# Retention, then a gated MLP, on one core: the fifth chunk of batch 0 loaded with the other four, and the first weight load issued one step sooner

## The chip, the core and the metric

The kernel runs on one core of one Trainium2 chip. The metric is the device time of one execution, in microseconds (us). The kernel before takes 321.57 us (median of three runs, 321.35 to 321.59). The profiled execution that all views below come from took 321.33 us.

## What is computed

Inputs are `q`, `k`, `v` (8 batches, 8 heads, 576 positions, 64 wide, all f32) and the weights `w_in` (512 x 2048) and `w_out` (2048 x 512). Cut to what matters:

```python
scores = scale * np.matmul(q, k.transpose(0, 1, 3, 2))
Dmat = np.where(rel >= 0, gamma[:, None, None] ** rel[None, :, :], 0.0)
ret = np.matmul(scores * Dmat[None, :, :, :], v)          # per batch and head
x = ret.transpose(0, 2, 1, 3).reshape(B * S, H * D)       # 4608 x 512
h = x @ w_in
out = (h * np.cos(h)) @ w_out                             # 4608 x 512, f32
```

## The kernel before

**Retention in chunks.** The 576 positions of a batch are cut into five chunks `r` = 0 to 4: four of 128 positions and a last one of 64. For each chunk, k and v are loaded from HBM in f32 to staging tiles (`load`; dst tiles `kn`, `vn`), k is cast to bf16 into `kqb` (`cast`, the instruction at L339) and v is multiplied by the decay into `vb` (`vmul`, L328). `turn_k` transposes a chunk of k on TensorE (PE) into a PSUM bank, and ACT or DVE copies it into `kqt` (L387). `turn_q` does the same for q. `scores` multiplies k by q into two PSUM banks, which DVE masks into `rt` (`mask`, L451). `rest` adds the output of the chunk in one PSUM bank from the running state `sb` and from `rt` and `vb`, updates the state in the bank `st` (copied by ACT to `sb`, L494), and copies the output to `xt` (L501). The outputs of all chunks stand one after another in `xt`, the input of the MLP.

**The MLP in blocks.** The 4608 tokens are cut into nine blocks `j` of 512. `mlp1(j, dt)` makes one of 16 slices of 128 hidden features: four matmuls, a sine on ACT (L526, the cosine), a product on DVE (L529). `mlp2` makes the output of 128 tokens in four parts of four matmuls each; part `p` reads the slices 4p to 4p+3 and the p-th quarter of `w_out`. `w_in` comes in four loads too, each for four values of `dt` (`WI`).

**Who loads what.** SP issues the k, v and q loads (`load`, L278; `load_q0`, L287) on one hardware queue (q1 in the profile). The weights and the q of batch 1 need a cast on the way, and POOL (GpSimd) issues them on its own queue (q0): `w_in_load` (L307), `w_out_load` (L314), `load_qx` (L301). Both queues feed the same 16 DMA engines. Each engine executes its instructions in program order, so a wait in POOL's or SP's list holds back all that stands behind it there.

**The order at the start** is written out by hand in `emit`. Block 0 of the MLP needs the tokens 0 to 511, the chunks 0 to 3 of batch 0. The fifth chunk of batch 0 is needed only by block 1 and is worked in between slices of `mlp1(0, dt)`: `turn_k(0, 4)` after dt 6, `scores(0, 4)` after dt 8, `rest(0, 4)` after dt 10. Before that, PE bridges waits with dummy matmuls (`spin`). SP's loads of chunk 4 wait for the first `w_in` load to have landed (`after=w[:1]`), and SP's loads of batch 1, which come next in SP's list, for the fourth (`after=w[3:]`). In POOL's list the two operations of chunk 4 (`casts(0, 4)`) stand between the four `w_in` issues and the four `w_out` issues; the casts of batch 1 follow the latter.

**PSUM banks.** There are eight: two for scores (`SC`), one for outputs (`PO`), one for the state (`ST`) and four (`MM`) which `bank()` hands out in turn. A group of matmuls that gets a bank waits until the last reader of the bank is done. PE has one instruction list, and a group waits at its first matmul for all that it reads and for its bank.

During block 0's `mlp2`, q, k of batch 1 are turned and its first chunks are worked (`turn_q(1, c)` after n = 7, `turn_k(1, 0)` after n = 9, and so on). From batch 2 on the transposes are DMA transposes (L350), and the loads run ahead of the compute.

Of the kernel before, what the change touches and what calls it, by code (L numbers as in the profile page):

```python
# [123 lines left out]
class _Kernel:  # L124
# [468 lines left out]
    def emit(self):  # L593
        s = self.s
        self.load("k", 0, 0)
        self.load_q0()
        for x, r in (("k", 1), ("v", 0), ("k", 2), ("v", 1), ("k", 3), ("v", 2), ("v", 3)):
            self.load(x, 0, r)
        self.consts_a()
        for c in range(NP):  # L600
            self.consts_b(c)
        self.consts_n()
        self.cast("pool", 0, 0)
        for c in range(NP):
            self.cast_q0(c)
        self.cast("pool", 0, 1)
        self.vmul("pool", 0, 0)
        self.cast("pool", 0, 2)
        self.vmul("pool", 0, 1)
        w = [self.w_in_load(0)]  # L610
        for r in (2, 3):
            self.vmul("pool", 0, r)
        for i in (1, 2, 3):
            w.append(self.w_in_load(i))

        for x in "kv":
            self.load(x, 0, 4, after=w[:1])
        self.casts(0, 4)
        for i in range(NWO):
            self.w_out_load(i)  # L620
            if i == 1:
                self.load_qx(1)

        po, st = (self.PO, self.bPO), (self.ST, self.bST)
        self.spin(30, po)
        self.turn_k(0, 0, st, "dve")
        for c in range(NP):
            self.turn_q(0, c)
            self.spin((8, 5, 5, 16)[c], po)
        self.scores(0, 0)  # L630
        self.turn_k(0, 1)
        self.spin(10, po)
        self.scores(0, 1, sc=[self.bank(), self.bank()])
        self.spin(8, po)
        self.turn_k(0, 2)
        self.rest(0, 0)
        self.scores(0, 2)
        self.cast("act", 0, 3)
        self.spin(6)
        self.rest(0, 1, self.bank(), "act")  # L640
        self.turn_k(0, 3, eng="dve")
        self.spin(8)
        self.scores(0, 3, sc=[self.bank(), self.bank()])
        self.rest(0, 2, eng="act")

        s.op("act", lambda e: e.activation(self.JUNK.ap(), self.C_PIH.ap(), AF.Sin), reads=[self.bC])
        self.spin(12)
        self.rest(0, 3, self.bank())
        self.spin(8, po)
        for r in range(NCH):  # L650
            for x in "kv":
                self.load(x, 1, r, after=w[3:])
        for r in range(NCH):
            self.casts(1, r)

        for dt in range(16):
            self.mlp1(0, dt)
            if dt == 6:
                self.turn_k(0, 4)
            if dt == 8:  # L660
                self.scores(0, 4)
            if dt == 10:
                self.rest(0, 4)

        self.fetch(2)
        for r in range(NCH):
            self.feed(2, r, 3 if r == NCH - 1 else 1)
        spare = [(self.PO, self.bPO), (self.SC[0], self.bSC[0]), (self.SC[1], self.bSC[1]),
                 (self.ST, self.bST)]
        for n in range(16):  # L670
            self.mlp2(0, n % 4, n // 4)
            if n == 7:
                for c in range(NP):
                    self.turn_q(1, c, spare[c])
            if n in (9, 11):
                self.turn_k(1, n // 11, spare[0])
            if n in (10, 13):
                self.scores(1, n // 13)
            if n == 14:
                self.rest(1, 0)  # L680
                self.turn_k(1, 2, self.bank())
        self.flush()
        self.rest(1, 1)
        self.spin(10)

        n = 3 * 64 + CH
        for dt in range(16):
            self.mlp1(1, dt, 0, n)
            if dt in (1, 7, 13):
                self.scores(1, 2 + dt // 6, True)  # L690
            if dt in (3, 9):
                self.turn_k(1, 3 + dt // 6)
            if dt in (5, 11):
                self.rest(1, 2 + dt // 6)
        for dt in range(16):
            self.mlp1(1, dt, n, TB - n)
        for j in range(1, NTB):
            b = j + 1
            for dt in range(16 if j > 1 else 0):
                self.mlp1(j, dt)  # L700
                if b < B_ and dt % 3 == 2:
                    self.feed(b, dt // 3)
            for n in range(16):

                if n == 0 and b <= B_:
                    self.rest(b - 1, NCH - 1)
                if b < B_:
                    if n == 0:
                        self.scores(b, 0)
                    elif n % 3 == 0 and n < 15:  # L710
                        self.stage(b, n // 3 - 1)
                if (j, n // 4) != (NTB - 1, 3):
                    self.mlp2(j, n // 4, n % 4)
        self.flush()
        self.last(NTB - 1, TB // 128 - 1)
        for name, (h, n) in s.dsem.items():
            if name[0] == "o":
                self.nc.scalar.wait_ge(h, n)
# [28 lines left out]
```

## Time and profile before

| What | Value |
|---|---|
| median of three runs | 321.57 us |
| the profiled execution: its own time / its span | 321.33 us / 319.6 us |
| TensorE clock granted | 1.00 |
| PE, DVE, ACT, POOL busy | 303.3, 176.6, 161.1, 106.8 us |
| first matmul of `mlp1(0, 0)` / of `mlp2(0, ...)` | 20.4 us / 38.9 us |
| DMA queues q1, q0, q10 (stores) | 57.0%, 9.2%, 8.9% of 16 engines' time over the span |
| HBM read / written | 36.70 MB / 9.44 MB |

The span runs from the first to the last instruction of the program; the 1.7 us between it and the execution's own time lie around the program. All times of the views count from the start of the span. "Busy" counts the time in which an engine executes, "idle before" the gap ahead of an instruction together with what ended it. A row of the timeline merges several instructions of one form (`x3`); some matmul records can be missing, so that a row says x2 where its neighbours say x3. The DMA issues show how long it took from an issue to the landing of the last byte.

### The profile page before, as it was taken

To read this page: it belongs to the slowest core of one execution; us is meant where nothing else is said; L and a number is where in the kernel's file an instruction comes from. 1 tells how busy PE (TensorE), PEld (TensorE's weight loads), DVE (VectorE), ACT (ScalarE), POOL (GpSimd) and SP (SyncE) were. 2 spreads that over 40 slices of the span, in tenths; PEclk is the share of its full clock that TensorE was granted. 3 is DMA by queue.
4 is the path that set the end of the run, shared out by engine and by line. 5 is a ranking of instruction groups with operands and counts; after the bars stand their busy time and mean duration, and the time that the engine had idled before them with its cause. 6 is when DMAs were issued, how large, how long until landed. Compare 5 with 4: busy or idle time off the path is not lost.

```text
span 319.6 us, 6480 instructions
## 1 busy us (share of the span) xinstructions
PE 303.3 (95%) x2530; PEld 161.4 (51%) x2566; DVE 176.6 (55%) x303; ACT 161.1 (50%) x294; POOL 106.8 (33%) x130
## 2 busy tenths in 40 slices
PE   6985997999999999999999999999999999999996
PEld 5752443667554455445544554455545554444444
DVE  3844823588554865476448743874388527504810
ACT  8374602788235824573357425842484337416811
POOL 4743512655656554555546454410000000000000
DMA  7998999999899999999999999921000100010012
GB/s 219 194 177 158 188 197 199 305 201 187 194 254 207 230 220 233 212 221 208 221 234 213 210 250 201 191 52 67 33 0 35 66 35 0 35 71 28 2 67 98
DMA packets 142430, 48.85 MB, mean 153 GB/s; under 512 B 132544, under 2 KB 137408, under 8 KB 142400
## 3 DMA queue, kind: packets, MB, share of 16 engines
q1 hardware_dynamic: 132464, 34.35, 57.0%
q0 software_dynamic: 4752, 4.78, 9.2%
q10 hardware_dynamic: 5184, 9.31, 8.9%
q8 instruction: 20, 0.33, 0.5%
q14 instruction: 10, 0.08, 0.1%
HBM read 36.70 MB, written 9.44 MB: 144 GB/s over the span
## 4 chain that ended last, share of the span: by engine, by line
PE 81%; DMA 11%; SPq 2%; issue 2%; POOL 2%; DVE 1%; ACT 0%
PE mm L424 53%; PE mm L426 18%; PE po L424 5%; DMA wout<-in_moe_w_out_dram 5%; PE sc L424 3%; DMA kn<-in_k_dram 3%; DMA win<-in_moe_w_in_dram 2%; DMA vn<-in_v_dram 2%; SPq L278 2%; PE st L424 1%; DVE gt L529 1%; POOL vb L328 1%; SPq L287 1%; POOL wout L314 0%; POOL qx L301 0%
## 5 line engine op out<-in xcount | busy, mean ns | idle before, releaser
L529 DVE TENSOR_TENSOR gt<-mm,cb 128x512 bf16<-128x512 f32 (+2 forms) x160 | 101.1, 637 | 69.8 <-ACT cb L526 66.5
L424 PE MATMUL mm<-xt,win 128*128 128x512 bf16 (+2 forms) x468 | 116.0, 357 | 1.4 <-DVE gt L529 0.5
L424 PE MATMUL mm<-wout,gt 128*128 128x512 bf16 (+1 forms) x426 | 112.1, 372 | 4.3 <-DMA wout<-in_moe_w_out_dram 2.1
L526 ACT ACTIVATE cb<-mm,c_pih 128x512 bf16<-128x512 f32 (+2 forms) x160 | 102.0, 645 | 27.1 <-PE mm L426 25.7
L424 PEld LDWEIGHTS mm<-xt,win 128*128 128x128 bf16 x480 | 44.8, 98 | 49.1 <-ACT cb L526 2.4
L424 PEld LDWEIGHTS mm<-wout,gt 128*128 128x128 bf16 x450 | 41.0, 98 | 46.9 <-DMA wout<-in_moe_w_out_dram 2.6
L426 PE MATMUL mm<-xt,win 128*128 128x512 bf16 (+2 forms) x160 | 57.2, 358 | 0.4
L426 PE MATMUL mm<-wout,gt 128*128 128x512 bf16 (+1 forms) x142 | 53.6, 378 | 0.5
L560 ACT ACTIVATE osb<-mm 128x512 f32<-128x512 f32 x35 | 20.9, 597 | 64.4 <-PE mm L426 64.4
L328 POOL TENSOR_TENSOR vb<-vn,wv 128x512 bf16<-128x512 f32 (+1 forms) x40 | 41.7, 1043 | 21.8 <-DMA vn<-in_v_dram 15.8
L451 DVE TENSOR_TENSOR rt<-sc,mk 128x512 bf16<-128x512 f32 (+1 forms) x76 | 44.5, 623 | 5.9 <-PE sc L426 5.9
L339 POOL CAST kqb<-kn 128x512 bf16<-128x512 f32 (+1 forms) x39 | 23.8, 611 | 63.8 <-DMA kn<-in_k_dram 61.9
L501 DVE CAST xt<-po 128x512 bf16<-128x512 f32 (+1 forms) x37 | 23.3, 630 | 39.1 <-PE po L426 39.0
L494 ACT ACTIVATE sb<-st 64x256 bf16<-64x256 f32 x64 | 24.2, 378 | 39.8 <-PE st L426 38.0
L328 POOL TENSOR_TENSOR kqb<-qn,upn 128x512 bf16<-128x512 f32 (+1 forms) x30 | 31.3, 1042 | 16.5 <-DMA qn<-in_q_dram 16.1
L426 PEld LDWEIGHTS mm<-xt,win 128*128 128x128 bf16 x160 | 15.6, 98 | 15.7
L426 PEld LDWEIGHTS mm<-wout,gt 128*128 128x128 bf16 x142 | 13.9, 98 | 16.5
L424 PE MATMUL po<-rt,vb 128*64 128x128 bf16 (+1 forms) x266 | 14.8, 220 | 0.0
L424 PE MATMUL sc<-kqt 64*128 64x128 bf16 (+1 forms) x266 | 14.3, 215 | 0.2 <-ACT kqt L387 0.2
L424 PEld LDWEIGHTS po<-rt,vb 128*64 128x64 bf16 (+1 forms) x266 | 9.1, 108 | 5.8 <-DVE rt L451 2.1
L424 PEld LDWEIGHTS po<-kqt,sb 128*128 128x128 bf16 x120 | 8.5, 98 | 6.8 <-DVE rt L451 0.6
L424 PE MATMUL po<-kqt,sb 128*128 128x128 bf16 (+1 forms) x120 | 10.8, 212 | 0.1
(94 smaller groups left out, 141.0 us busy)
## 6 DMA issues: line engine op xcount, KB each, us to landing
out_dram<-osb ACTq DMA_DIRECT2D x35, 256.0 KB, 3.2
kn<-in_k_dram SPq DMA_DIRECT2D x32, 256.0 KB, 4.5
vn<-in_v_dram SPq DMA_DIRECT2D x32, 256.0 KB, 5.2
qn<-in_q_dram SPq DMA_DIRECT2D x24, 256.0 KB, 4.7
win<-in_moe_w_in_dram POOLq DMA_DIRECT2D x4, 512.0 KB, 6.9
wout<-in_moe_w_out_dram POOLq DMA_DIRECT2D x4, 512.0 KB, 13.8
qn<-in_q_dram SPq DMA_DIRECT2D x4, 288.0 KB, 4.9
kn<-in_k_dram SPq DMA_DIRECT2D x8, 128.0 KB, 3.4
```

Of the source, the lines that this page charges most:

```text
L278: return self.s.dma(eng, f"{x}n{r}", lambda e: e.dma_start(dst, src), writes=[self.bST32[x][r]], after=after)
L287: s.dma("sp", f"q0_{c}", lambda e: e.dma_start(dst, src), writes=[self.bQN[c]])
L328: self.s.op(eng, lambda e: e.tensor_tensor(bass.AP(t, o, [[pitch, ck], [D_, H_], [1, D_]]), self.staged(x, r, [[D_, H_], [1, D_]]), bass.A ...
L339: fn = (lambda e: e.activation(o, f, AF.Copy)) if eng == "act" else (lambda e: e.tensor_copy(o, f))
L424: self.nc.tensor.matmul(o, a, b, **kw)
L426: return s.done("pe", self.nc.tensor.matmul(o, a, b, **kw), reads, writes)
L451: self.s.op("dve", lambda e: e.tensor_tensor(bass.AP(self.RT[k][hp], 0, p3), bass.AP(sc[0], 0, p3), bass.AP(self.MK, 0, [[CH, ck], [0, NP] ...
L494: s.op("act", lambda e: e.activation(bass.AP(self.SB[r % 2], 64 * hp * 512 + 64 * hp, [[512, 64], [128, NP], [1, D_]]), bass.AP(self.ST, 6 ...
L501: fn = (lambda e: e.activation(o, f, AF.Copy)) if eng == "act" else (lambda e: e.tensor_copy(o, f))
L526: s.op("act", lambda e: e.activation(co, mo, AF.Sin, bias=self.C_PIH.ap(), scale=1.0), reads=[bm, self.bC], writes=[bcb])
L529: s.op("dve", lambda e: e.tensor_tensor(bass.AP(g, dt * TB + o, [[16 * TB, 128], [1, n]]), mo, co, ALU.mult), reads=[bm, bcb], writes=[bg])
L560: s.op("act", lambda e: e.activation(o.ap(), m.ap(), AF.Copy), reads=[bm], writes=[bo])
```

## The change

Three things are moved, and the same work is done as before.

- SP's loads of chunk 4 of batch 0 follow the loads of chunk 3 at once, without the wait for `w_in`.
- In POOL's list the first `w_in` issue moves ahead of `vmul(0, 1)`, the second ahead of `vmul(0, 3)`; `casts(0, 4)` moves behind all weight issues. On PE the chunk is worked four slices later (after dt 10, 12 and 14).
- The four `MM` banks of batch 0's chunks are named instead of drawn in turn: `scores(0, 3)` takes banks 2 and 3 instead of 0 and 1, `rest(0, 1)` bank 0, `turn_k(0, 3)` bank 1, `rest(0, 3)` bank 0. The dummy matmuls ahead of `scores(0, 3)` are 14 in `PO` instead of 8 in an `MM` bank, the last 8 use bank 1 instead of `PO`, and `mlp1` starts with bank 1.

```diff
-        for x, r in (("k", 1), ("v", 0), ("k", 2), ("v", 1), ("k", 3), ("v", 2), ("v", 3)):
+        for x, r in (("k", 1), ("v", 0), ("k", 2), ("v", 1), ("k", 3), ("v", 2), ("v", 3),
+                     ("k", 4), ("v", 4)):
             self.load(x, 0, r)
...
         self.cast("pool", 0, 2)
-        self.vmul("pool", 0, 1)
-        w = [self.w_in_load(0)]
-        for r in (2, 3):
+        self.w_in_load(0)
+        for r in (1, 2):
             self.vmul("pool", 0, r)
-        for i in (1, 2, 3):
-            w.append(self.w_in_load(i))
-
-        for x in "kv":
-            self.load(x, 0, 4, after=w[:1])
-        self.casts(0, 4)
+        self.w_in_load(1)
+        self.vmul("pool", 0, 3)
+        self.w_in_load(2)
+        w = self.w_in_load(3)
         for i in range(NWO):
             self.w_out_load(i)
             if i == 1:
                 self.load_qx(1)
+        self.casts(0, 4)
...
+        mm = list(zip(self.MM, self.bMM))
         self.scores(0, 0)
-        self.turn_k(0, 1)
+        self.turn_k(0, 1, mm[0])
         self.spin(10, po)
-        self.scores(0, 1, sc=[self.bank(), self.bank()])
+        self.scores(0, 1, sc=mm[1:3])
         self.spin(8, po)
-        self.turn_k(0, 2)
+        self.turn_k(0, 2, mm[3])
         self.rest(0, 0)
         self.scores(0, 2)
         self.cast("act", 0, 3)
-        self.spin(6)
-        self.rest(0, 1, self.bank(), "act")
-        self.turn_k(0, 3, eng="dve")
-        self.spin(8)
-        self.scores(0, 3, sc=[self.bank(), self.bank()])
+        self.spin(6, mm[0])
+        self.rest(0, 1, mm[0], "act")
+        self.turn_k(0, 3, mm[1], "dve")
+        self.spin(14, po)
+        self.scores(0, 3, sc=mm[2:4])
         self.rest(0, 2, eng="act")
...
-        self.spin(12)
-        self.rest(0, 3, self.bank())
-        self.spin(8, po)
+        self.spin(12, mm[1])
+        self.rest(0, 3, mm[0])
+        self.spin(8, mm[1])
+        self.n_mm = 1
         for r in range(NCH):
             for x in "kv":
-                self.load(x, 1, r, after=w[3:])
+                self.load(x, 1, r, after=[w])
...
-            if dt == 6:
+            if dt == 10:
                 self.turn_k(0, 4)
-            if dt == 8:
+            if dt == 12:
                 self.scores(0, 4)
-            if dt == 10:
+            if dt == 14:
                 self.rest(0, 4)
```

## The prediction, made before the result was known

> **What bounds the kernel now.** First the page: is one engine the bound, and does it idle?
>
> ```profile
> PE 303.3 (95%) x2530; PEld 161.4 (51%) x2566; DVE 176.6 (55%) x303; ACT 161.1 (50%) x294; POOL 106.8 (33%) x130
> ```
>
> PE works 303.3 of 319.6 us, so an edit gains time only where PE idles and nothing later takes the gain back. Second, PE's waits, for the first 60 us and then for the rest (what waited, for what: us in total, times, longest):
>
> ```profile
> PE mm L424 <- POOL kqb L339: 3.2, 1, 3.2
> PE mm L424 <- DMA wout<-in_moe_w_out_dram: 2.1, 1, 2.1
> ...
> PE mm L424 <- ACT xt L501: 0.7, 1, 0.7
> PE mm L424 <- DVE xt L501: 0.3, 1, 0.3
> ```
> ```profile
> PE mm L424 <- issue: 1.7, 11, 0.2
> PE mm L424 <- DVE gt L529: 0.7, 3, 0.3
> ```
>
> From 60 us on PE waits 2.4 us in all, and for no transfer. What the first 60 us lose reaches the end unchanged. Third, POOL's timeline (start, us, instruction, idle before it and what ended it), because the longest wait names a POOL cast:
>
> ```profile
> 11.71 0.61 POOL L339 CAST kqb<-kn 128x512 bf16<-128x512 f32 x1
> 13.25 1.05 POOL L328 TENSOR_TENSOR vb<-vn,wv 128x512 bf16<-128x512 f32 x1 [0.93 <-DMA vn<-in_v_dram]
> 14.23 0.92 POOL L307 DMA_DIRECT2D win<-in_moe_w_in_dram  x1
> 15.25 2.03 POOL L328 TENSOR_TENSOR vb<-vn,wv 128x512 bf16<-128x512 f32 x2
> 17.23 2.29 POOL L307 DMA_DIRECT2D win<-in_moe_w_in_dram  x3
> 29.07 0.60 POOL L339 CAST kqb<-kn 64x512 bf16<-64x512 f32 x1 [9.55 <-DMA kn<-in_k_dram]
> 29.69 1.03 POOL L328 TENSOR_TENSOR vb<-vn,wv 64x512 bf16<-64x512 f32 x1
> 30.68 1.54 POOL L314 DMA_DIRECT2D wout<-in_moe_w_out_dram x2
> ```
>
> POOL sits 9.55 us for k of chunk 4. Its load was issued at 20.12, when the first w_in load had landed, and took 8.9 us (DMA issues). The cast ends at 29.67, PE resumes at 29.82, and the w_out issues queue behind it. Fourth, the windows (PE, PEld, DVE, ACT, POOL busy, clock, DMA share, GB/s):
>
> ```profile
> 15.00:16.00 1.00, 1.00 (x26) 0.85 (x21) 0.78 (x2) 0.64 (x2) 0.91 (x2) 1.00 0.27 38
> 16.00:17.00 1.00, 0.28 (x10) 0.21 (x8) 0.35 (x1) 0.71 (x2) 1.00 (x2) 1.00 0.65 89
> 29.00:30.00 1.00, 0.18 (x4) 0.18 (x4) 0.00 (x0) 0.00 (x0) 0.92 (x2) 1.00 0.04 8
> 30.00:31.00 1.00, 1.00 (x9) 0.50 (x6) 0.00 (x0) 0.38 (x1) 1.00 (x2) 1.00 0.17 41
> ```
>
> The DMA engines are full in nearly all the first 53 us, but for two holes, 15.3 to 17.0 and 28.7 to 31.0: 4.0 us. The first lies between v of chunk 3 and the first w_in load, the second between the fourth w_in load and w_out.
>
> **Part 1, chunk 4.** PE's last matmul before the stall starts at 26.23. Matmuls of 512 columns follow each other every 0.22 us, so the next could have started at 26.45; it started at 29.82: **3.37 us**. In the new kernel `turn_k(0, 4)` comes at about 29.5 (below). Chunk 4 is in SP's list right behind v of chunk 3 (issued 11.75 to 12.85), and on POOL behind the nine issues: cast(0, 2) ends at 12.32; w_in 0 takes 0.92 (its row); vmul 1 runs 13.25 to 14.30 as now; vmul 2 waits for v of chunk 2 (landed 15.17), to 16.27; w_in 1 to 17.05; vmul 3 to 18.10; w_in 2 and 3, four w_out and qx are seven issues of 0.76, to 23.4; the cast to 24.0, vmul 4 to 25.1. Cover: 5.5 us. What POOL queues behind it, the casts of batch 1, waits for loads that are still to come.
>
> **Part 2, w_out.** Stalls of the same kind follow: at 42.40 to 42.67 for w_out 1 (0.27), at 46.14 to 46.23 for qx (0.09), at 47.55 to 49.48 for w_out 2 (1.93; the row at 49.70 counts two matmuls of three, so the group began a beat earlier). Sum **2.29 us**. Do they go, when PE arrives 6 us sooner? That is a sum over packets. A w_in or w_out load is 512 packets of 1 KB, a whole k or v load 1024 of 256 B (the size over the packet's). Rates: q0 alone 789 packets in 20 to 24 us, 197 per us; both together, 40 to 48 us:
>
> ```profile
> q0 software_dynamic: 1206, 1.26, 91.8%
> q1 hardware_dynamic: 1207, 0.30, 28.7%
> ```
>
> One to one, 151 per us each. An issue needs 2.2 us to full flow (14.23 to 16.4); behind q1's backlog 2.6 (30.68 to 33.3). So w_in 0, issued at 12.30, flows from about 15.0. Chunk 4's 1024 packets run beside it to 21.8, and q0 passes w_in 0 by 18.4 and w_in 1 by 21.8; then 197 per us: w_in 2 24.4, w_in 3 27.0, w_out 0 29.6. Landing is 0.7 later (v of chunk 3: last packets 15.3, landed 15.90). Batch 1's loads start when w_in 3 has landed, 27.7, and q1's packets then come 4 us later, as they did at 20.12 (none of q1 in 20 to 24). From 31.7 at 151: w_out 1 32.4, qx 35.8, w_out 2 39.1, w_out 3 42.5.
>
> With `mlp1` starting at 20.02, each slice 0.865: dt 4 needs w_in 1 at 23.5 (lands 22.5), dt 8 w_in 2 at 26.9 (25.1), dt 12 w_in 3 at 30.6 (27.7); `turn_k(0, 4)` at 29.5; `mlp2` begins at 35.1 (w_out 0 30.3), n = 4 at 38.6 (33.1), qx at 42.0 (36.5), n = 8 at 43.3 (39.8), n = 12 at 47.5 (43.2). Tightest is w_in 1 with 1.0 us. Batch 1: q1 has 1630 packets through by 42.5, k 0 among them, and alone it moves some 950 per us (14 to 15 us): v 0 lands at 43.6, k 1 at 44.7, k 2 at 46.9; `turn_k(1, 1)` comes at 47.3 and needs the cast of k 1, 45.3 at the latest. Covered. From batch 2 on, scores come 7.7 to 12.1 us after their transposes have landed (batch 2: 79.73 after 67.64, 94.37 after 86.67), more than the gain.
>
> **Part 3, banks and start.** `scores(0, 3)` waited 0.72 us, to 16.79, for the bank which ACT emptied (the xt copy 16.14 to 16.74). Its new banks are empty by 13.7. Next late is its `kqt` copy on DVE, 15.66 to 16.35; 14 dummies from 15.46 at 0.056 each end at 16.25. So it starts at 16.41: **0.38 us** sooner. It stays: the state copy of `rest(0, 2)` moves along (18.81 to 18.43), `rest(0, 3)` to 18.48, the xt copy to 19.96, `mlp1` from 20.40 to 20.02 (the row at 20.62 also lacks one matmul). vmul 3, ready at 18.10, has 0.38 to spare. w_in 0 must land by 19.97: 5.87 us as in its own row gives 18.2, 8.13 as for w_out 0 20.43; my packets say 19.1. If 20.43, the gain is zero. The turn, scores and rest of chunk 4 and the dummies are the same matmuls at another place: nothing.
>
> **Sum:** 3.37 + 2.29 + 0.38 = 6.04 us. The profiled execution, 321.33, becomes 315.3; the median stands 0.24 above it, so **315.5 us**.
>
> **A rule weighed.** Does w_in 0 slow v of chunk 3, which `rest(0, 3)` needs? At 14.5 some 598 packets of q1 are left. In the trace a queue that comes late gets little at first: from 33 to 35 us, when w_out 0 joined, q1 moved 893 packets and q0 155. So v of chunk 3 passes by 16.3 and lands by 17.0, in time for vmul 3. The Trainium skill, "DMA: Bandwidth & Descriptors", section "Queues, rings and completion order", has each engine alternate between its queues packet by packet; the steady 1206 to 1207 agrees, the 893 to 155 does not. By the rule alone v of chunk 3 would be slowed from the first packet, and the time would be that of the second case below.
>
> **The rivals.**
> 1. *v of chunk 3 late:* at 151 per us from 14.5 the 598 packets end at 18.5, landed 19.1; vmul 3 to 20.1, `rest(0, 3)` 1.3 later than now: 321.57 - 5.66 + 1.3 = 317.2. For it: the even split of the steady state. Against: 893 to 155. Chance 0.12.
> 2. *The engines stay the bound:* as many k and v packets as now go ahead of w_out 2, which then comes only 4.0 us sooner, the two holes: 317.6. Of this kind too: w_in 1 late, which w_out 1's 11.16 us from issue to landing would put at 27.4, 3.9 after its need: 319.4 at worst. For it: DMA shares above 1 all along. Against: batch 1's loads are now asked for after w_out, not before. Chance 0.18.
> 3. *Slower: POOL is held at its issues.* Up to seven of its loads will be under way at once; the trace shows five (none of 30.68 to 34.45 landed before 38.81), at 0.76 each. If POOL stops for the ring, chunk 4's cast, now last, waits. Held to five, the last issue waits for w_in 3 and the cast ends at 29.1, in time. From 29.5 each us costs one; 35.5 is the point from which the kernel is slower. Chance 0.04.
> 4. *Nothing gained* (stalls reappear in full later): 0.02, 321.6.
>
> **How the numbers follow.** Forecast 0.64. Range 314.9 to 317.9: below, the whole 0.72 of the bank wait instead of 0.38, and 0.24 between runs; above, the first rival and most of the second. Faster by over 0.2% (about what a measurement can tell here) 0.94, within it 0.02, slower 0.04.
>
> **What would show it.** Right: PE's wait for POOL L339 gone, no wait for wout, `mlp1` at 20.0, `mlp2` at 35.1, no DMA hole at 15 or 29 us. Wrong: POOL's L314 issues longer than 0.8 us, vmul 3 waiting for vn past 17.4, or a PE wait for win.

## The result, and the profile after

The changed kernel takes 319.93 us (median of 11 runs, 318.32 to 321.12) against 321.57 (11 runs): a ratio of 0.9943, 95% interval 0.9918 to 0.9968. It is faster, as forecast, but by 1.6 us and not by 6, and its runs scatter over 2.8 us. The profiled execution took 321.02 us (span 319.3), 1.1 us above the median, with a mean granted clock of 0.995. So the views below show one of the changed kernel's longer executions.

PE's waits in the first 60 us of the changed kernel (waited for: us in total, times, longest), the counterpart of the four lines shown of before:

```profile
PE mm L424 <- POOL vb L328: 4.1, 1, 4.1
...
PE mm L424 <- POOL qx L291: 0.7, 3, 0.3
PE mm L424 <- issue: 0.4, 2, 0.2
PE sc L424 <- ACT kqt L387: 0.2, 1, 0.2
```

The waits for chunk 4's cast, for w_out and for ACT's xt copy are gone, all three. In their place stands one wait of 4.1 us for a product of v. POOL's timeline says which (start, us, instruction, idle before it and what ended it):

```profile
12.32 0.92 POOL L307 DMA_DIRECT2D win<-in_moe_w_in_dram  x1
13.58 1.03 POOL L328 TENSOR_TENSOR vb<-vn,wv 128x512 bf16<-128x512 f32 x1 [0.34 <-DMA vn<-in_v_dram]
15.19 1.04 POOL L328 TENSOR_TENSOR vb<-vn,wv 128x512 bf16<-128x512 f32 x1 [0.57 <-DMA vn<-in_v_dram]
16.17 0.80 POOL L307 DMA_DIRECT2D win<-in_moe_w_in_dram  x1
21.61 1.03 POOL L328 TENSOR_TENSOR vb<-vn,wv 128x512 bf16<-128x512 f32 x1 [4.64 <-DMA vn<-in_v_dram]
22.59 1.54 POOL L307 DMA_DIRECT2D win<-in_moe_w_in_dram  x2
24.13 1.49 POOL L314 DMA_DIRECT2D wout<-in_moe_w_out_dram  x2
25.59 0.77 POOL L301 DMA_DIRECT2D qx<-in_q_dram  x1
26.32 1.52 POOL L314 DMA_DIRECT2D wout<-in_moe_w_out_dram  x2
27.79 0.67 POOL L339 CAST kqb<-kn 64x512 bf16<-64x512 f32 x1
```

The row at 21.61 is vmul 3. It waits for v of chunk 3, which was issued at 12.09 as before (11.75) but landed at 21.52, not at 15.90. PE's timeline of the changed kernel, with the start of each group in the first column:

```profile
17.85 0.79 PE L424 MATMUL mm<-ident 128*128 128x128 bf16 x11
...
22.78 0.39 PE L424 MATMUL mm<-kqt,sb 128*128 128x128 bf16 x4 [4.08 <-POOL vb L328]
...
24.82 1.06 PE L424 MATMUL mm<-xt,win 128*128 128x512 bf16 x2 [0.22 <-issue]
...
26.10 1.26 PE L424 MATMUL mm<-xt,win 128*128 128x512 bf16 x3
...
27.41 0.81 PE L424 MATMUL mm<-xt,win 128*128 128x512 bf16 x3
...
28.28 0.81 PE L424 MATMUL mm<-xt,win 128*128 128x512 bf16 x3
...
49.38 0.59 PE L424 MATMUL mm<-wout,gt 128*128 128x512 bf16 x2 [0.16 <-issue]
```

The rows of the kernel before that answer to the first slice of `mlp1` and to the last row, the ninth group of `mlp2`:

```profile
20.62 0.59 PE L424 MATMUL mm<-xt,win 128*128 128x512 bf16 x2 [0.34 <-DVE xt L501]
...
49.70 0.59 PE L424 MATMUL mm<-wout,gt 128*128 128x512 bf16 x2 [2.15 <-DMA wout<-in_moe_w_out_dram]
```

`rest(0, 3)` begins at 22.78, and `mlp1` at 24.39 where it began at 20.40 before. (Each of the rows marked x2 lacks its first matmul; at 24.82 the matmuls stand 0.43 us apart, in the others 0.22.) The first two slices take 1.71 and 1.31 us, not 0.865. The windows say why (the stretch and its length, busy time of PE, PEld, DVE, ACT and POOL, then the granted clock, the DMA share and GB/s):

```profile
14.00:15.00 1.00, 0.94 (x18) 0.66 (x14) 1.00 (x3) 0.95 (x3) 0.61 (x1) 1.00 0.65 125
23.00:24.00 1.00, 1.00 (x25) 0.86 (x22) 0.45 (x1) 0.32 (x1) 1.00 (x2) 0.79 0.28 45
24.00:25.00 1.00, 0.78 (x7) 0.70 (x7) 0.25 (x1) 0.43 (x2) 1.00 (x3) 0.50 0.78 45
25.00:26.00 1.00, 1.00 (x3) 0.30 (x2) 0.00 (x0) 0.00 (x0) 1.00 (x2) 0.50 1.11 183
26.00:27.00 1.00, 1.00 (x4) 0.35 (x3) 0.00 (x0) 0.65 (x1) 1.00 (x2) 0.50 1.23 198
27.00:28.00 1.00, 1.00 (x6) 0.47 (x5) 0.69 (x1) 0.42 (x2) 1.00 (x3) 1.00 1.24 203
```

After 4.1 idle us the TensorE clock was granted at half for 3.4 us. The balance of the two profiles closes: `mlp1` begins 4.0 us later, its first three slices lose 1.3 (28.28 minus 24.39 is 3.89, against 2.59), and the two stalls behind it are gone: from the start of `mlp1` to the ninth group of `mlp2` the new kernel needs 24.8 us (24.39 to 49.16, the 1.3 included), the old one 29.1 (20.40 to 49.49). That leaves 0.3 us in all, the difference of the spans.

### The profile page after: what moved, and what is told of

It is laid out like the page before. It is cut to its first block, busy times and chain, and to the rows that moved or that the text cites. A ratio compares the mean times of both kernels' runs of the same rounds, so it can differ in the third digit from the quotient of the medians.

```text
span 319.3 us, 6492 instructions
## 1 busy us (share of the span) xinstructions
PE 305.7 (96%) x2536; PEld 162.9 (51%) x2572; DVE 176.5 (55%) x303; ACT 160.9 (50%) x294; POOL 106.8 (33%) x130
## 4 chain that ended last, share of the span: by engine, by line
PE 89%; SPq 3%; DMA 3%; issue 2%; DVE 1%; ACT 1%; POOL 0%
PE mm L424 59%; PE mm L426 20%; PE po L424 6%; PE sc L424 4%; DMA vn<-in_v_dram 3%; SPq L278 3%; PE st L424 1%; DVE gt L529 1%; SPq L287 1%; ACT cb L526 1%; POOL vb L328 0%; DVE rt L451 0%; ACT osb L579 0%; PE po L426 0%; PE sc L426 0%
## 5 line engine op out<-in xcount | busy, mean ns | idle before, releaser
L560 ACT ACTIVATE osb<-mm 128x512 f32<-128x512 f32 x35 | 20.9, 597 | 64.4 <-PE mm L426 64.4
L426 PEld LDWEIGHTS mm<-wout,gt 128*128 128x128 bf16 x142 | 13.9, 98 | 16.5
```

Of the source, the lines that this page charges most:

```text
L426: return s.done("pe", self.nc.tensor.matmul(o, a, b, **kw), reads, writes)
L560: s.op("act", lambda e: e.activation(o.ap(), m.ap(), AF.Copy), reads=[bm], writes=[bo])
```

## The experiments

**Theory A:** w_in 0, issued 1.9 us sooner, joins the DMA engines while v of chunk 3 still stands in the other queue and starves it; PE then waits, and the idle wait costs the clock as well. **Theory B:** the packets of chunk 4, put right behind v of chunk 3 in its own queue, are what delays it.

**1. w_in 0 back.** The changed kernel with one line moved.

```diff
-        self.w_in_load(0)
-        for r in (1, 2):
-            self.vmul("pool", 0, r)
+        self.vmul("pool", 0, 1)
+        self.w_in_load(0)
+        self.vmul("pool", 0, 2)
```

> The changed kernel with one line moved: the first w_in issue again behind vmul 1 on POOL, some 1.9 us later (near 14.3); chunk 4's early loads and the banks as changed. Theory A (the early issue of w_in 0 meets v of chunk 3 still in its queue and starves it, 4.1 us of PE wait for vb and a halved TensorE clock after it): v of chunk 3 lands by 17, no PE wait for vb over 0.5 us, clock 1.00, mlp1 begins at 20.3 to 21, time 315.3 to 316.5. Theory B (chunk 4's 1024 packets right behind v of chunk 3 are what delays it): v of chunk 3 still lands at 19 or later, PE waits 2 us or more, time 318 to 320.

316.87 us (316.52 to 319.31; ratio 0.9873, 0.9818 to 0.9928). v of chunk 3 landed at 16.71, the clock stayed at 1.00. PE's waits of this kernel:

```profile
...
PE mm L424 <- POOL qx L291: 1.2, 1, 1.2
PE mm L424 <- DVE xt L501: 0.4, 1, 0.4
...
```

No wait for vb: A, against B. The time lies 0.4 us above the expected end of the range. w_in 0, with chunk 4's packets beside it, took 7.1 us to land (5.87 before), at 21.43, and `mlp1` began at 21.6. In this execution the first q load was late as well (the 1.2 us), so the two can't be told apart here.

**2. Chunk 4 gated again, w_in 0 early.**

```diff
-                     ("k", 4), ("v", 4)):
...
-        self.w_in_load(0)
+        w0 = self.w_in_load(0)
...
+        for x in "kv":
+            self.load(x, 0, 4, after=[w0])
         self.casts(0, 4)
```

> The changed kernel with chunk 4's k and v loads again waiting for the first w_in load; the early w_in issue, the late casts of chunk 4 and the banks stay. Theory A: v of chunk 3 still lands late (18.5 to 21.5, without chunk 4's packets in the queue perhaps the earlier end), PE waits 1.5 to 4 us for vb, time 317.5 to 320. Theory B: v of chunk 3 lands by 17, no wait for vb, time 315 to 316.5.

318.57 us (316.15 to 321.44; 0.9866 to 0.9943). v of chunk 3 landed at 19.88 without any packet of chunk 4 behind it, and PE waited 2.7 us for vb. Again A, not B, in that execution, which took 319.63. The median stands between two groups, though: five executions with a mean granted clock of 1.00 took 316.15 to 317.51, five with 0.995 or less 319.63 to 321.44 (3.4 us at half clock take 0.005 off the mean). Some executions seem to pay little for the early w_in 0; no trace of one of them was kept.

**3 and 6. Dummies through the wait,** to keep PE busy: 84, and then 56, instead of 12.

```diff
-        self.spin(12, mm[1])
+        self.spin(84, mm[1])
```

> The changed kernel with 84 dummy matmuls instead of 12 ahead of rest(0, 3), so that PE is busy while v of chunk 3 is awaited; nothing else. Theory A, second half (the idle 4.1 us cost the granted clock, 0.5 from 24 to 27 us, and this costs 1.2 to 1.8 us on top of the wait): clock 1.00 throughout, mlp1's slices 0.865 from the first, time 1.2 to 1.8 us below the changed kernel, 318 to 318.7. Rival (the clock column costs nothing, mlp1 waits for w_in 0 anyway): within 0.4 us of the changed kernel, near 320.

319.25 us (318.79 to 321.06; 0.9914 to 0.9960). Above the range expected. The granted clock was 1.00 in all runs and the slices of `mlp1` stood 0.86 us apart from the first on. But vmul 3 was done at 20.04 in this execution and the dummies kept PE to 22.1: they outlasted the wait by 2 us.

> The changed kernel with 56 dummy matmuls instead of 12 ahead of rest(0, 3), which end near 20.6 us; 84 had ended 2 us after the awaited product was ready. Theory A (the idle wait costs the clock, some 1.1 to 1.5 us): clock 1.00 in the profile, the first slices of mlp1 0.865 us apart, time 318.2 to 318.9. Rival (the clock costs nothing): 319.5 to 320.2.

319.08 us (318.12 to 320.06; 0.9901 to 0.9957), again above the range. Here too the slices stood 0.86 apart. The dummies outlasted the wait again: in the profiled execution, the longest of the four (320.06), `rest(0, 3)` began at 22.05, 1.2 us after the end of vmul 3 at 20.89. There the clock was granted at half from 8 to 11 us already, ahead of all that is compared here, and the start came late. Both medians are below the changed kernel's by 0.7 and 0.85 us, but the intervals overlap. So the loss to the clock, 1.3 us in the profile of the changed kernel, is seen in the trace; in the times it isn't settled.

**4. Chunk 4 alone:** the kernel before with the first part of the change.

```diff
+                     ("k", 4), ("v", 4)):
...
-        for x in "kv":
-            self.load(x, 0, 4, after=w[:1])
-        self.casts(0, 4)
         for i in range(NWO):
             self.w_out_load(i)
             if i == 1:
                 self.load_qx(1)
+        self.casts(0, 4)
...
-            if dt == 6:
+            if dt == 10:
                 self.turn_k(0, 4)
```

(`scores` and `rest` move to 12 and 14 likewise.)

> The kernel before with the first part of the change alone: chunk 4 loaded right behind chunk 3, its casts behind all weight issues, its work four slices later. The w_in issues and the banks as before. Theory A: gain of the two stalls, 3.4 plus 2.3 us, less at most 0.5 for w_in 0 beside chunk 4's packets: 315.7 to 316.4; no PE wait for POOL or wout over 0.3 us. Theory B: v of chunk 3 lands at 19 or later, time 318 to 320.

317.15 us (316.65 to 318.72; ratio 0.9878, 0.9820 to 0.9935): 4.3 us by itself by the medians (the interval, from four runs, reaches from 2.1 to 5.8), 0.75 above the range. v of chunk 3 landed at 16.58, and no wait for POOL's cast or w_out is left. A new one is:

```profile
PE mm L424 <- DMA win<-in_moe_w_in_dram: 1.9, 1, 1.9
```

w_in 0, issued at 14.04, landed at 21.60, after 7.6 us and not 5.87. Chunk 4's early loads are paid for by w_in 0.

**5. Both out of the way:** w_in 0 back as in 1, and chunk 4's loads gated as in 2.

```diff
-        self.w_in_load(0)
-        for r in (1, 2):
-            self.vmul("pool", 0, r)
+        self.vmul("pool", 0, 1)
+        w0 = self.w_in_load(0)
+        self.vmul("pool", 0, 2)
...
+        for x in "kv":
+            self.load(x, 0, 4, after=[w0])
         self.casts(0, 4)
```

> The first w_in issue back behind vmul 1, and chunk 4's loads waiting for the first w_in load again; the late casts of chunk 4, its later work on PE, and the banks as changed. Theory A (each load pays for what stands beside it in the other queue: v of chunk 3 for w_in 0, and w_in 0 for chunk 4, 7.1 to 7.6 us to landing with chunk 4 beside it against 5.87 without): w_in 0 lands within 6.2 us of its issue, v of chunk 3 by 16.5, chunk 4 by 29.5, no PE wait over 0.5 us after 20 us, time 315.3 to 316.2, 0.7 to 1.5 us below the kernel with the early loads (316.87). Rival C (chunk 4's loads beside w_in 0 cost nothing at the end, the profile's differences lie in the scatter of the first loads): 316.6 to 317.2. Rival D (chunk 4 now comes too late for its turn after slice 10): a PE wait of 0.5 to 2 us for the cast of k, 316.5 to 318.

316.55 us (316.28 to 317.35; ratio 0.9848, 0.9830 to 0.9865), the lowest median of all, though its interval overlaps those of 1, 4, 11 and 12. w_in 0 landed 5.6 us after its issue, v of chunk 3 at 16.23, and `mlp1` began at 20.4. But two waits appeared:

```profile
PE po L424 <- POOL kqb L339: 0.9, 1, 0.9
...
PE mm L424 <- DMA win<-in_moe_w_in_dram: 0.4, 1, 0.4
```

It is only 0.3 us below experiment 1, not 0.7 to 1.5: the time misses A's range, lies just below C's and fits D's, though D's wait, for chunk 4, isn't among those found. The second w_in load, now beside chunk 4, landed at 24.28; batch 1's loads, let go by the fourth at 30.75, brought k of batch 1's second chunk at 48.76, and the cast of that is the 0.9 us.

**7. The banks alone** (the third part of the change put into the kernel before).

```diff
-        self.scores(0, 3, sc=[self.bank(), self.bank()])
+        self.scores(0, 3, sc=mm[2:4])
...
-        self.rest(0, 3, self.bank())
+        self.rest(0, 3, mm[0])
```

> The kernel before with the named banks alone. Theory (the step of 0.38 us in the prediction): scores(0, 3) begins 0.3 to 0.45 us sooner against the scores before it, the 0.72 us wait for ACT gone, and mlp1 begins at the later of 20.0 and the landing of w_in 0, near 20.1; the chunk-4 wait then holds as before, since k of chunk 4 lands at 29.0 whatever PE does: gain 0, 321.2 to 321.8. Rival (the 0.38 us reach the end): 320.9 to 321.1.

321.38 us (ratio 0.9996, 0.9977 to 1.0015): nothing, as expected. The 0.72 us wait is gone, PE then waits 0.5 us for w_in 0 and still 3.1 for chunk 4's cast.

**8. v of chunk 3 on a queue of its own:** issued by ACT, the rest as changed.

```diff
-        for x, r in (("k", 1), ("v", 0), ("k", 2), ("v", 1), ("k", 3), ("v", 2), ("v", 3),
+        for x, r in (("k", 1), ("v", 0), ("k", 2), ("v", 1), ("k", 3), ("v", 2),
                      ("k", 4), ("v", 4)):
...
         self.consts_n()
+        self.load("v", 0, 3, "act")
```

> The changed kernel with one load moved to another queue: v of chunk 3 is issued by ACT near 7.6 us, not by SP behind v of chunk 2; w_in 0 stays early. Theory A (v of chunk 3 is late because it is still in q1 when w_in 0 joins): it lands by 14, no PE wait for vb over 0.5 us; the loads of chunks 1 to 3 on SP's queue come up to 0.9 us later; w_in 0, beside chunk 4's packets, lands at 19.5 to 21; time 315.8 to 317.3. Rival (w_in 0's early traffic delays whatever is under way, by bytes and not by the queue's order): another load takes its place, PE waits 1.5 us or more for a k or v product before 20 us, time 318 to 320.

317.71 us (317.16 to 317.84; 0.9868 to 0.9899), 0.4 above the range. ACT issued it sooner than thought, at 3.03; it landed at 10.28, and the loads of chunks 1 and 2 came 0.8 to 1.6 us later, so that w_in 0 was issued at 13.90. The load that was then caught beside it is v of chunk 4, 8.3 us to landing, which nothing needs until much later. PE waits 1.1 us for k casts, but for no vb. As a test of A this fell flat: w_in 0 did not stay early, and with w_in 0 issued at 14.0 to 14.7 v of chunk 3 was on time on SP's queue too. The rival's half, that something else pays, is what the profile shows: w_in 0, 8.4 us to landing, was there at 22.31, and `mlp1` began at 22.45, 0.9 us after PE was free.

**10. w_in 0 sooner, alone** (in the kernel before).

```diff
-        self.vmul("pool", 0, 1)
         w = [self.w_in_load(0)]
-        for r in (2, 3):
+        for r in (1, 2, 3):
```

> The kernel before with the sooner w_in 0 issue alone (ahead of vmul 1); chunk 4 and the banks as before. Theory A: v of chunk 3 again lands late, 18.5 to 21.5, PE waits 1.5 to 4 us for vb ahead of mlp1; but chunk 4's k, issued when w_in 0 has landed near 19.5, lands near 28.5 as before, so the later start only eats into the 3.4 us that PE waits for it: time 320.8 to 322.5, the same within noise. Rival (the sooner issue is a gain by itself): v of chunk 3 on time, mlp1 at 20.0, 320 to 321.

319.06 us (317.60 to 325.19; ratio 0.9941, 0.9912 to 0.9971): a miss, it is faster by 2.3 us. The first half came as expected: v of chunk 3 took 8.7 us and landed at 20.89, PE waited 3.2 us for its product, the clock fell to half. The second half did not. POOL's timeline:

```profile
20.95 1.04 POOL L328 TENSOR_TENSOR vb<-vn,wv 128x512 bf16<-128x512 f32 x1 [4.76 <-DMA vn<-in_v_dram]
21.94 2.29 POOL L307 DMA_DIRECT2D win<-in_moe_w_in_dram  x3
24.20 0.64 POOL L339 CAST kqb<-kn 64x512 bf16<-64x512 f32 x1
```

POOL, held by vmul 3, had not yet issued the next w_in loads when chunk 4's k was asked for at 20.74. With the engines empty it landed 2.8 us later, not 8.9, so POOL never waited for it and w_out left 4.9 us sooner than before (25.80 against 30.68). The same load takes 2.8 us or 9 by what stands in the other queue.

**9, 11 and 12. Can the rest be had?** Experiment 5 with later gates for its two waits; chunk 4's work on PE comes later too (in 9 after slices 12 and 14 and the second part of `mlp2`, in 11 after slices 12, 14 and 15).

```diff
-        self.w_in_load(1)
+        w1 = self.w_in_load(1)
...
-        self.w_in_load(2)
-        w = self.w_in_load(3)
+        w = self.w_in_load(2)
+        self.w_in_load(3)
...
-            self.load(x, 0, 4, after=[w0])
+            self.load(x, 0, 4, after=[w1])
```

> The kernel with the first w_in issue back and chunk 4 gated (316.55), with its two remaining waits aimed at: chunk 4's loads wait for the second w_in load instead of the first (PE waited 0.4 us for the second), batch 1's loads for the third instead of the fourth (PE waited 0.9 us for a cast of batch 1), and chunk 4's work on PE comes after slices 12 and 14 and after the second part of mlp2. Theory A (every one of these waits is a transfer that stood beside another): both waits gone, 315.2 to 316.0. Rival (the engines are full, so that one late transfer is traded for another): a wait of 0.5 us or more appears for chunk 4's cast or for w_out, 316.2 to 317.2.

361.64 us (361.00 to 362.04). This kernel tells nothing of the theories: its `rest(0, 4)` came to stand behind the recording of batch 2's casts into the same `kqb` and `vb` tiles, so chunk 4 of batch 0 was computed from batch 2's data, and PE waited 42.8 us for batch 2's DMA transpose.

> The intent of the run before last, with chunk 4's last step after slice 15 of mlp1, ahead of all that touches its tiles again: first w_in issue behind vmul 1, chunk 4's loads wait for the second w_in load, batch 1's for the third, chunk 4 worked after slices 12, 14 and 15. Theory A (each wait that was left at 316.55 us is a transfer that stood beside another): the 0.4 us wait for w_in and the 0.9 us wait for a cast of batch 1 are gone, 315.2 to 316.0. Rival (full engines, one late transfer is traded for another): a new wait of 0.5 us or more for chunk 4's cast or for w_out, 316.2 to 317.2.

317.80 us (316.64 to 318.41; 0.9861 to 0.9906), more than the rival's range too. Both aimed-at waits are gone, and chunk 4, landed at 32.5 and 36.4, brings others:

```profile
PE mm L424 <- ACT sb L494: 1.1, 1, 1.1
PE po L424 <- DVE rt L451: 1.0, 1, 1.0
PE mm L424 <- DVE gt L529: 0.7, 1, 0.7
```

These groups wait for several things, and the engine named had long been done. Read against the landings, the first ended with w_in 0 (landed 21.12, `mlp1` from 21.25), the second and third with vmul 4 (done at 37.48, PE at 37.63) and chunk 4's cast (33.17 and 33.32).

Experiment 12 is experiment 5 with the second of the three edits, batch 1's gate, alone.

> The 316.55 us kernel (first w_in issue back, chunk 4 waiting for the first w_in load) with batch 1's loads waiting for the third w_in load instead of the fourth, and nothing else. Theory A: the 0.9 us wait for a cast of batch 1 goes, the 0.4 us wait for w_in stays: 315.6 to 316.2. Rival: w_out, now beside batch 1's packets for longer, comes late, PE waits for it 0.5 us or more, 316.4 to 317.2.

317.19 us (316.17 to 317.75; 0.9831 to 0.9881): the rival's. Batch 1's loads were asked for 4.0 us sooner (26.77 against 30.77), but k of the second chunk landed at 49.26, no sooner: while w_out was under way q1 moved one packet for each of q0's (607 to 610 from 38 to 42 us), and the last of w_out landed at 47.70. PE waited 1.3 us for its cast and 0.5 for w_out. None of the three has a lower median than experiment 5.

## Why the prediction was wrong, point by point

**Right: the sign, and the first two parts.** Chunk 4's wait is gone, its cast ended at 28.5 with `turn_k` at 35.3. The w_out waits are gone. From the start of `mlp1` to the ninth group of `mlp2` the new kernel needs what was forecast (29.1 less 5.66, 23.4 us) but for the 1.3 us of the clock.

**Wrong: the step "A rule weighed".** It asked the right question, whether w_in 0 slows v of chunk 3, and answered from the wrong row. It read 893 to 155 (33 to 35 us) as "a queue that comes late gets little at first", and let v of chunk 3 land by 17.0. But those 2 us are the join itself, and their sum hides what came of it. The kernel before, 33.0 to 33.5 and then 34.5 to 35.0:

```profile
q1 hardware_dynamic: 412, 0.10, 103.7%
q0 software_dynamic: 2, 0.00, 2.4%
...
q1 hardware_dynamic: 88, 0.02, 29.1%
q0 software_dynamic: 67, 0.07, 85.6%
```

Within 2 us q1 had fallen from 412 packets per half us to 88; a load still in the queue at that point is slowed almost fivefold. The queues' counts over the first 2 us after w_in 0 came, 14.5 to 16.5, in the changed kernel:

```profile
q0 software_dynamic: 152, 0.16, 58.0%
q1 hardware_dynamic: 530, 0.13, 35.0%
```

q0 got what it had got at 33 us, 152 against 155, but q1 moved 530 and not 893: from 14.0 on the engines were not full (share 0.65 in 14 to 15), and from 16 to 18 the split was one to one (283 to 275). The sign that the prediction itself had named as wrong, vmul 3 waiting for vn past 17.4, came: it began at 21.61. Over the one traced execution of each kernel with v of chunk 3 on SP's queue, the issue time of w_in 0 separates the two outcomes, with or without chunk 4: issued at 11.5 to 12.5 (the changed kernel, experiments 2, 3, 6, 10), it landed at 18.9 to 21.5; at 14.0 to 14.7 (before, experiments 1, 4, 5, 7, 11, 12), at 15.6 to 16.7. In the early ones v of chunk 3 landed 0.2 to 1.5 us behind w_in 0 itself. The first rival, given 0.12, was the mechanism; the one-to-one split of the Trainium skill ("DMA: Bandwidth & Descriptors", section "Queues, rings and completion order"), weighed and set aside, was nearer to the truth. It isn't the whole of it: in experiment 3 q0 moved 197 packets from 14.5 to 15.5 and q1 none. (The prediction says that by the rule the time would be that of its "second case"; v of chunk 3 late is its first rival, 317.2.)

**Undersized: the first rival itself.** Its 19.1 for the landing became 21.52 in the profiled execution and 18.9 to 20.9 in the four other kernels with an early w_in 0, and it had no term for the clock. Its time, 317.2, was below all 11 runs; the range ended at 317.9.

**Not seen: w_in 0 pays too.** The estimate 19.1 for its landing became 21.12 (8.8 us), and 7.1 and 7.6 us in experiments 1 and 4, where chunk 4's loads stood right behind v of chunk 3, against 5.6 to 6.4 in those where chunk 4 was asked for later (before, 5, 7, 11, 12). Among the kernels with an early w_in 0 it took 6.0 to 8.8, in experiment 10 8.5 without chunk 4, so chunk 4 isn't all of it there. By the medians part 1 is worth 4.3 us and not 5.7: the early loads that remove one wait push the start of `mlp1` from 20.4 to 21.7. The second rival, engines that stay the bound, is right in this: the six kernels that cure the wait for vb in different ways (1, 4, 5, 8, 11, 12) all end between 316.5 and 317.8, and the profile of each has another transfer late, though w_out, which it had named, in experiment 12 alone (0.5 us). The third, POOL held at its issues, did not come: in the changed kernel seven loads of POOL's were under way at 27.1, and each issue took 0.74 to 0.79 us.

**Part 3** came as a mechanism: the wait of 0.72 us is gone. Alone it gains nothing (experiment 7): the wait for chunk 4's cast behind it ends when it did before. Two stalls in series hid each other as well in experiment 10: a start 3.9 us later cost nothing, since the wait for chunk 4 behind it vanished.

**Open:** why q1 slowed from 14.0 on (289 packets to 14.5, where the kernel before had 483), ahead of the first q0 packets, and why the landing scatters by 2.6 us between the five executions with an early w_in 0. The counts here are sums over the 16 DMA engines; the single engines are not in these views.

## What to carry to other kernels

Before an issue is moved forward, list what stands in the other queues at its new time and who waits for it: here the load under way was slowed, and the moved one with it. A wait can be the cover of the next one, as in experiments 7 and 10, so try each part of such a change alone. Where the engines are full, moving a load early is a choice of which operand comes late, and the one to choose is the one needed last.

## What the runs showed of the hardware that was not expected

- v of chunk 3 (256 KB in 1024 packets of 256 B), which took 3.7 to 4.9 us from issue to landing on SP's queue, took 7.0 to 9.4 when a load with 1 KB packets was issued on another queue between 0.4 us before and 0.3 us after it. The order of the issues alone doesn't settle it: v of chunk 4, half the size, took 3.8 us in experiment 1, issued 0.1 us ahead of w_in 0, and 8.3 in experiment 8, 0.3 behind it. k of chunk 4, of that size too, took 2.8 us on empty engines (experiment 10) and 8.4 to 9.0 behind queued w_in loads (before, 5, 7, 11, 12).
- Waits of PE of 4.1 us (the changed kernel), 3.2 (experiment 10) and 2.7 (experiment 2) were each followed by 3.4 us at a granted clock of 0.50; the wait of 3.2 us at 26.6 in the kernel before was not (1.00 in every window). The Trainium skill, "TensorE: Matmul & The Clock Gate", Part 1, puts the drop after an idle window of about 3.4 us which runs freely. That fits the 4.1 us and the kernel before; the waits of 3.2 in experiment 10 and of 2.7 are below it, and there the measurement decides.
